# Block 2's keys: cast by Pool on landing, turned before the last weight group, that group loaded in two parts

## The chip, the cores and the metric

One Trainium2 chip, of which the kernel uses one core. The metric is the device time of one execution in microseconds (us). TensorE is called PE here, VectorE DVE, ScalarE ACT, GpSimd POOL or Pool, and SyncE SP. "SPq" and "POOLq" are the queues on which SP and Pool issue transfers (DMAs).

## What is computed

Chunked attention over 4 batches, 8 heads, 768 positions and a head width of 64, then a dense layer pair with a gate. Cut to what matters:

```python
for c in range(24):                      # chunks of 32 queries
    k_ctx = k[:, :, l_start:r_end]       # 16 positions to the left, 8 to the right
    k_full = concat([mem_k, k_ctx]); v_full = concat([mem_v, v_ctx])   # 8 memory rows ahead
    a = softmax(q_c @ k_full.T / 8)
    out[:, :, c_start:c_end] = a @ v_full
x = out.transpose(0, 2, 1, 3).reshape(3072, 512)
return (relu(x @ w_gate) * (x @ w_val)) @ w_out      # 512 -> 1536 -> 512
```

Inputs and output are float32; the kernel works in float16 and accumulates in float32.

## The kernel before, in words

The 3072 rows are cut into eight blocks of 384, two to a batch. For each block the kernel loads keys and queries (`load_kq`, L153: `kraw`, for even blocks also the memory and edge rows `kx`, then `qraw`), casts them to float16 (`cast3`, L169, into `kn` and `qn`; `cast_kx`, L175), turns them with a transposing DMA (`turn_k`, L183, into `kT`; `turn_q`, L189, into `qT`), and lets Pool copy the turned keys into bands of 120 (`bands`, L193, into `kb`: six copies for an even block). Then come four attention steps (`Step`, L231): scores on PE (L252), the exponential on ACT (L259), a mask on DVE, the values on PE (L270, which read `vb`), a division on DVE, and a transposing DMA of the result into `xT`. The dense layer of a block is twelve units `dff` (L315: four gate matmuls, a relu on ACT, four value matmuls, a product on DVE) and three output tiles.

Blocks 0 and 1 are begun together by a list written out by hand (`ORDER`, L466). After it stands the stage that the change touches (L586 to L625): 28 units for blocks 0 and 1, counted by u. Units 0 to 7 are dense units on the weight columns 512 to 1023, four for each block. Units 8 to 15 are those on columns 1024 to 1535: 8 to 11 of block 0, 12 to 15 of block 1, with a 128-column slice each, so that units 8 and 9 read columns 1024 to 1279 and units 10 and 11 columns 1280 to 1535. Units 16 to 27 are output tiles in halves (`outp_part`, L336): 16 to 21 need the first half of `w_out` (`load_wo(0)`), 22 to 27 the second (`load_wo(1)`). Into these units block 2's attention is woven: scores of steps 0 and 1 ahead of unit 12, of steps 2 and 3 ahead of unit 17 (`su`); values within units 14, 15, 19 and 20 (`vu`).

`manual_schedule` keeps each engine's instructions in program order, so the order of the text is the order of each queue. What is prepared for blocks 2 and 3 hangs on the units in the table `hook` (L591): a call that is entered at u stands behind that unit's own instructions. Ahead of the table stand a Pool write into `kraw` that waits for the weight columns up to 1023 (L586), `load_kq(2)` on SP, `cast_kx` on Pool, and `load_w(1024, 512)` on Pool: the last weight group, one DMA for `w_gate_sb` and one for `w_val_sb`, which cast to float16 on the way. Pool also issues `load_vb` (L163, block 2's values, a DMA for the rows and one for the memory rows of each step) and `load_wo` (L452, three DMAs of four row chunks each). So Pool's queue holds weight loads, value loads, band copies and output weights in one line, and what stands behind a waiting band copy waits with it.

After the 28 units a loop runs blocks 2 to 7 (L629), each with the attention of the next block woven in.

Of the kernel before, what the change touches and what calls it, by code (L numbers as in the profile page):

```python
# [15 lines left out]
def kernel(  # L16
# [57 lines left out]
    dv, pl = dve.tensor_copy, pool.tensor_copy  # L74
# [63 lines left out]
    def load3(eng, c, n, h0=0, nh=H):  # L138
        t = {"k": k, "q": q, "v": v}[c]
        i = n % 2  # L140
        dst = (vlong if c == "v" else raw[c])[:, i, h0:h0 + nh].rearrange("p h t d -> p h (t d)")
        src = bass.AP(tensor=t.tensor, offset=t[n // 2, h0, MB * i, 0].offset,
                      ap=[[R3 * D, 128], [S * D, nh], [1, R3 * D]])
        eng.dma_start(dst, src)  # L144
# [4 lines left out]
    def kx_rows(eng, b, d, t, mem, eng2=None):  # L149
        eng.dma_start(d[0:NMEM], mem[b].rearrange("h n d -> n h d"))  # L150
        (eng2 or eng).dma_start(d[NMEM:2 * NMEM], rows(t, b, MB, NMEM))

    def load_kq(n):  # L153
        load3(sp, "k", n)
        if n % 2 == 0:
            kx_rows(sp, n // 2, kx[:, (n // 2) % 2], k, mem_k)
        load3(sp, "q", n)
# [5 lines left out]
    def load_vb(n, j):  # L163
        pool.dma_start(vb_t[n % 2][0:BAND, j, :, 0:D], rows(v, n // 2, starts[NJ * (n % 2) + j], BAND))
        pool.dma_start(vb_t[n % 2][BAND:128, j, :, 0:D], mem_v[n // 2].rearrange("h n d -> n h d"))
# [3 lines left out]
    def cast3(eng, c, n, a0=0, na=HP):  # L169
        i = n % 2  # L170
        d = (kn[:, i, 0:R3].rearrange("p t a c -> p a t c") if c == "k" else qn[:, i])[:, a0:a0 + na]
        eng(d.rearrange("p a t (x d) -> p a x t d", x=2),  # L172
            raw[c][:, i, 2 * a0:2 * a0 + 2 * na].rearrange("p (a x) t d -> p a x t d", x=2))

    def cast_kx(eng, b):  # L175
        eng(kn[0:2 * NMEM, 0, R3], kx[:, b % 2].rearrange("p (a x) d -> p a (x d)", x=2))
# [6 lines left out]
    def turn_k(n):  # L183
        i = n % 2
        nt = R3 + 1 - i
        sp.dma_start_transpose(kT_t[i][:, 0:nt].rearrange("p t a c -> p (t a) c"),
                               kn[:, i, 0:nt].rearrange("p t a c -> p (t a c)"))

    def turn_q(n):  # L189
        i = n % 2  # L190
        sp.dma_start_transpose(qT_t[i].rearrange("p a t c -> p (a t) c"), qn[:, i].rearrange("p a t c -> p (a t c)"))

    def bands(n, eng, part=range(6)):  # L193
        i = n % 2
        kT, kb = kT_t[i], kb_t[i]
        early = n in EARLY

        def src(t, off, dims, sa=128):
            return bass.AP(tensor=t.tensor, offset=t.offset + off, ap=[t.ap[0], [sa, HP]] + dims)

        def dst(j, off, dims):
            return bass.AP(tensor=kb.tensor, offset=kb.offset + 128 * j + off, ap=[kb.ap[0], [NJ * 128, HP]] + dims)

        nj, TS = 3 - i, HP * 128
        P = QB // R3 - 6
        for r, t in enumerate((2, 0, 1)):
            if r in part:
                eng(dst(1, r, [[128, nj], [R3, 40]]), src(kT, TS * t + P + (r > 0), [[PP, nj], [1, 40]]))  # L208
        if 3 in part:
            if i == 0:  # L210
                eng(dst(0, 0, [[R3, 40], [1, R3]]), src(kT, 0, [[1, 40], [TS, R3]]))
            else:
                e, es, eo, ea = (ke, HP * NMEM, 2, NMEM) if early else (kT_t[0], TS, 122, 128)
                eng(dst(0, 16, [[R3, 35], [1, R3]]), src(kT, 0, [[1, 35], [TS, R3]]))
                eng(dst(0, 0, [[1, 1]]), src(e, 2 * es + eo, [[1, 1]], ea))
                eng(dst(0, 1, [[R3, 5], [1, R3]]), src(e, eo + 1, [[1, 5], [es, R3]], ea))
        if 4 in part and i == 1:
            eng(dst(3, 0, [[R3, 40], [1, R3]]), src(kT, 88, [[1, 40], [TS, R3]]))
        if 5 in part:
            if i == 0:  # L220
                eng(dst(3, 112, [[1, NMEM]]), src(kT, R3 * TS + NMEM, [[1, NMEM]]))
            if early:
                eng(dst(0, BAND, [[128, NJ], [1, NMEM]]), src(kb_t[0], BAND, [[0, NJ], [1, NMEM]], NJ * 128))  # L223
            else:
                eng(dst(0, BAND, [[128, NJ], [1, NMEM]]), src(kT_t[0], R3 * TS, [[0, NJ], [1, NMEM]]))
# [221 lines left out]
    def load_w(c0, w, only=None):  # L447
        for i, (s_, d_) in enumerate(((moe_w_gate, w_gate_sb), (moe_w_val, w_val_sb))):
            if only in (None, i):
                pool.dma_start(d_[:, :, c0:c0 + w], s_.rearrange("(c p) f -> p c f", p=128)[:, :, c0:c0 + w])  # L450

    def load_wo(x):  # L452
        for c in range(0, NDC, 4):
            pool.dma_start(w_out_sb[:, c:c + 4, HC * x:HC * x + HC],
                           moe_w_out.rearrange("(c p) f -> p c f", p=128)[:, c:c + 4, HC * x:HC * x + HC])
# [6 lines left out]
    ac = act.copy  # L462
# [117 lines left out]
    def att(n):  # L580
# [4 lines left out]

    pl(raw["k"][0:1, 0, 0, 0, 0:1], w_gate_sb[0:1, 0, 1023:1024])  # L586
    load_kq(2)
    cast_kx(pl, 1)
    load_w(1024, 512)

    hook = {  # L591
        0: [lambda: cast3(ac, "k", 2, 0, 2)],
        1: [lambda: cast3(ac, "k", 2, 2, 2), lambda: turn_k(2)],
        3: [lambda: load_vb(2, 0), lambda: load_vb(2, 1), lambda: load_wo(0)],
        4: [lambda: cast3(ac, "q", 2, 0, 2)],
        5: [lambda: cast3(ac, "q", 2, 2, 2), lambda: turn_q(2), lambda: load_kq(3), lambda: bands(2, pl)],
        8: [lambda: load_vb(2, 2), lambda: load_vb(2, 3)],
        10: [lambda: load_wo(1)],
        12: [lambda j=j: load_vb(3, j) for j in range(NJ)],
# [100 lines left out]
```

## Time and profile before

| | |
|---|---|
| seven runs | median 238.33 us, 238.05 to 241.1 |
| the profiled execution | 238.33 us, of it 236.6 us span |
| granted PE clock, mean | 0.991 |
| PE busy | 225.3 us (95% of the span) |
| DVE, ACT, POOL busy | 107.9, 113.6, 62.0 us |
| DMA | 38.62 MB, 163 GB/s over the span |
| `kn<-kraw` cast, 128x768 | POOL 827 ns (one), ACT 832 ns (median of 13), DVE 638 ns (median of 2) |
| `kT<-kn` issue on SP | 1.49 to 5.44 us, six of them |
| `w_out_sb` DMA, issue to landing | 7.5 to 14.3 us, median 10.5 |

The span runs from the first instruction to the last, and the rest of a run's time lies around it. "Busy" counts pipelined matmuls, so PE's 95% doesn't say that it works at its peak; what the time of a stretch is worth is read from the gaps in PE's timeline and from the granted clock of the stretch. A timeline row has the start, the duration, engine, line, operation and tiles, and in brackets how long the engine had been idle before it and what released it. A row of DMA queues has packets, MB and the share of 16 engines; q1 is the queue on which SP issues (q1 of the hardware kind), q0 that of Pool (software). In the trace's packet records the kinds of transfer can be told by their packet size: 256 bytes for a transposing DMA, 768 for keys and queries, 128 for block 2's values, 1024 or 512 for weights.

### The profile page before, as it was taken

How to read it: one execution, taken by the hardware profiler on the slowest of the kernel's cores; microseconds unless marked ns; L12 is line 12 of the kernel's file. 1: busy time of each engine (PE TensorE's matmuls, PEld its weight loads, DVE VectorE, ACT ScalarE, POOL GpSimd, SP SyncE). 2: the span in 40 equal slices, each digit the busy share in tenths (PEclk: the TensorE clock that was granted, in tenths of full speed). 3: DMA queues.
4: the chain of work that ended last, by engine and by line, in shares of the span. 5: the costliest groups of instructions: out<-in, count | busy, mean ns of one | idle time of the engine just before them, and what ended most of it. 6: DMA issues, size and time to landing. Idle time of an engine off the chain costs nothing.

```text
span 236.6 us, 4765 instructions
## 1 busy us (share of the span) xinstructions
PE 225.3 (95%) x1819; PEld 137.2 (58%) x1819; DVE 107.9 (46%) x231; ACT 113.6 (48%) x201; POOL 62.0 (26%) x115
## 2 busy tenths in 40 slices
PE   7989899992999999999999999999999999999994
PEld 5656666651589856645665556545654566556543
DVE  5378745440542037622764057704861276414410
ACT  2386655641354546634573465454664355133312
POOL 6589408409680321006000320005000500000000
PEclk9999999999799999999999999999999999999999
DMA  6999999999999999459972999289935901220012
GB/s 173 321 268 178 201 224 190 169 157 224 243 161 155 247 249 248 84 114 235 305 144 43 230 302 194 42 193 260 258 73 129 173 1 36 64 102 1 3 44 90
DMA packets 91883, 38.62 MB, mean 163 GB/s; under 512 B 64308, under 2 KB 89652, under 8 KB 91860
## 3 DMA queue, kind: packets, MB, share of 16 engines
q1 hardware_dynamic: 73868, 32.53, 59.4%
q0 software_dynamic: 17920, 5.77, 24.9%
q8 instruction: 14, 0.23, 0.4%
q14 instruction: 9, 0.07, 0.1%
q10 hardware_dynamic: 72, 0.02, 0.0%
HBM read 30.24 MB, written 6.29 MB: 154 GB/s over the span
## 4 chain that ended last, share of the span: by engine, by line
PE 85%; DMA 9%; DVE 2%; SPq 1%; ACT 1%; issue 1%; ACTq 0%; DVEq 0%
PE PS L300 51%; PE PS L330 19%; PE PS L339 8%; DMA qT<-qn 5%; PE PS L270 3%; DMA vraw<-in_v_dram 3%; PE PS L252 3%; DMA kraw<-in_k_dram 2%; SPq L144 1%; DVE x_big L279 1%; PE PS L288 0%; PE PS L246 0%; ACT ex L259 0%; PE PS L395 0%; DVE kb L223 0%
## 5 line engine op out<-in xcount | busy, mean ns | idle before, releaser
L311 DVE TENSOR_TENSOR gvT<-PS,g_relu 128x384 f16<-128x384 f32 x96 | 53.2, 554 | 100.6 <-PE PS L300 98.7
L300 PE MATMUL PS<-xT,w_val_sb 128*128 128x384 f16 x384 | 78.3, 328 | 0.5 <-ACT xT L291 0.5
L300 PE MATMUL PS<-xT,w_gate_sb 128*128 128x384 f16 x384 | 78.7, 329 | 0.0
L305 ACT ACTIVATE g_relu<-PS 128x384 f16<-128x384 f32 x96 | 47.2, 491 | 54.1 <-PE PS L300 42.4
L300 PEld LDWEIGHTS <-w_gate_sb 128*128 128x128 f16 x384 | 36.8, 99 | 24.9 <-issue 0.8
L300 PEld LDWEIGHTS <-w_val_sb 128*128 128x128 f16 x384 | 36.6, 98 | 23.7 <-issue 1.5
L330 PE MATMUL PS<-w_out_sb,gvT 128*128 128x512 f16 x204 | 45.8, 379 | 0.0
L208 POOL COPY kb<-kT 128x320 f16<-128x320 f16 (+1 forms) x19 | 14.8, 871 | 97.9 <-DMA kT<-kn 76.4
L330 PEld LDWEIGHTS <-gvT 128*128 128x128 f16 x204 | 19.6, 98 | 22.3
L259 ACT ACTIVATE ex<-PS 128x768 f16<-128x768 f32 x32 | 25.6, 809 | 10.9 <-PE PS L252 10.9
L333 ACT COPY o_sb<-PS 128x512 f32<-128x512 f32 x17 | 9.9, 585 | 35.0 <-PE PS L330 35.0
L279 DVE TENSOR_TENSOR x_big<-PS,rinv 96x512 f16<-96x512 f32 x32 | 22.0, 686 | 1.1
L339 PE MATMUL PS<-w_out_sb,gvT 128*128 128x256 f16 (+2 forms) x168 | 19.2, 273 | 0.0
L339 PEld LDWEIGHTS <-gvT 128*128 128x128 f16 x168 | 16.1, 98 | 2.4
L270 PEld LDWEIGHTS <-ex 128*128 128x128 f16 x256 | 12.2, 98 | 5.0 <-issue 0.7
L270 PE MATMUL PS<-vb,ex 128*128 128x66 f16 x256 | 13.4, 194 | 0.6 <-DVE x_big L279 0.5
L252 PE MATMUL PS<-qT,kb 64*128 64x96 f16 x256 | 8.9, 206 | 4.6 <-DMA qT<-qn 4.6
L252 PEld LDWEIGHTS <-kb 64*128 64x128 f16 x256 | 6.2, 95 | 10.3 <-issue 6.2
L266 DVE TENSOR_TENSOR ex<-ex,mask_int 128x768 f16<-128x768 f16 x19 | 10.3, 562 | 1.8 <-ACT ex L259 1.7
L172 ACT CAST kn<-kraw 128x768 f16<-128x768 f32 x13 | 10.8, 829 | 0.6 <-DMA kraw<-in_k_dram 0.6
L172 ACT CAST qn<-qraw 128x768 f16<-128x768 f32 x13 | 10.8, 833 | 0.0
L342 ACT COPY o_sb<-PS 128x256 f32<-128x256 f32 (+2 forms) x14 | 5.2, 372 | 10.4 <-PE PS L339 9.7
(103 smaller groups left out, 126.7 us busy)
## 6 DMA issues: line engine op xcount, KB each, us to landing
kraw<-in_k_dram SPq DMA_DIRECT2D x7, 768.0 KB
qraw<-in_q_dram SPq DMA_DIRECT2D x7, 768.0 KB
vraw<-in_v_dram SPq DMA_DIRECT2D x20, 240.0 KB
out_dram<-o_sb SPq DMA_DIRECT2D x17, 256.0 KB
w_out_sb<-in_moe_w_out_dram POOLq DMA_DIRECT2D x6, 256.0 KB, 10.5
out_dram<-o_sb SPq DMA_DIRECT2D x12, 128.0 KB
w_gate_sb<-in_moe_w_gate_dram POOLq DMA_DIRECT2D x2, 512.0 KB, 7.3
w_val_sb<-in_moe_w_val_dram POOLq DMA_DIRECT2D x2, 512.0 KB, 9.4
```

The source lines that it names most:

```text
L172: eng(d.rearrange("p a t (x d) -> p a x t d", x=2), raw[c][:, i, 2 * a0:2 * a0 + 2 * na].rearrange("p (a x) t d -> p a x t d", x=2))
L208: eng(dst(1, r, [[128, nj], [R3, 40]]), src(kT, TS * t + P + (r > 0), [[PP, nj], [1, 40]]))
L252: pe.matmul(o.rearrange("p (t c) -> p t c", t=R3), lhsT=self.kb[r, a, j, :], rhs=qT_t[i][r, a, :, PP * j:PP * j + PP], start=not self.pm, ...
L259: act.activation(self.ex[:, :, 0:QB].rearrange("p (h b) c -> p b h c", b=2), PS[:, self.sb:self.sb + 2, 0:HP * QB].rearrange("p b (h c) -> ...
L266: dve.tensor_tensor(out=e, in0=e, in1=m8, op=ALU.mult)
L270: pe.matmul(PS[:, self.pb + h // 4, VW * (h % 4):VW * (h % 4) + VW], lhsT=self.ex[:, h, :], rhs=self.vb[:, self.j, h, :], start=True, stop ...
L279: dve.tensor_tensor(out=self.x.rearrange("p (b h d) -> p b h d", b=2, h=4), in0=o[:, :, :, 0:D], in1=rb, op=ALU.mult)
L300: pe.matmul(o, lhsT=w_sb[:, f, 128 * m:128 * m + 128], rhs=xTs[n][:, f, c0:c0 + w], start=(f == 0), stop=(f == NFC - 1))
L305: act.activation(g_relu, g_ps, ACT.Relu)
L311: dve.tensor_tensor(out=gvT[n][:, m].rearrange("p (t j c) -> p t j c", t=R3, j=NJ)[:, :, j0:j0 + nj], in0=vl_ps.rearrange("p (j t c) -> p ...
L330: pe.matmul(PS[:, o], lhsT=gvT[n][:, m, 128 * t:128 * t + 128], rhs=w_out_sb[:, m, :], start=(m == 0), stop=(m == NDC - 1))
L339: pe.matmul(o, lhsT=gvT[n][:, m, 128 * t:128 * t + 128], rhs=w_out_sb[:, m, c0:c1], start=(m == 0), stop=(m == NDC - 1))
```

## The change

Pool, not ACT, casts block 2's keys, as soon as they have landed. The turning DMA of the keys is issued by SP after these casts and that of `kx`, and in Pool's queue the weight group's loads come after the casts: first columns 1024 to 1279 of both weights, then 1280 to 1535. The band copies of block 2 stand directly behind these loads, ahead of `load_vb(2, 0)`, `load_vb(2, 1)` and `load_wo(0)`. ACT casts the queries behind units 0 and 1, where it cast the keys before; behind unit 1, not 5, stand the turning DMA of the queries and the loads of block 3's keys and queries. PE's and DVE's instructions and their order stay as they were.

```diff
     pl(raw["k"][0:1, 0, 0, 0, 0:1], w_gate_sb[0:1, 0, 1023:1024])
     load_kq(2)
+    cast3(pl, "k", 2, 0, 2)
+    cast3(pl, "k", 2, 2, 2)
     cast_kx(pl, 1)
-    load_w(1024, 512)
+    turn_k(2)
+    load_w(1024, 256)
+    load_w(1280, 256)
+    bands(2, pl)
 
     hook = {
-        0: [lambda: cast3(ac, "k", 2, 0, 2)],
-        1: [lambda: cast3(ac, "k", 2, 2, 2), lambda: turn_k(2)],
+        0: [lambda: cast3(ac, "q", 2, 0, 2)],
+        1: [lambda: cast3(ac, "q", 2, 2, 2), lambda: turn_q(2), lambda: load_kq(3)],
         3: [lambda: load_vb(2, 0), lambda: load_vb(2, 1), lambda: load_wo(0)],
-        4: [lambda: cast3(ac, "q", 2, 0, 2)],
-        5: [lambda: cast3(ac, "q", 2, 2, 2), lambda: turn_q(2), lambda: load_kq(3), lambda: bands(2, pl)],
         8: [lambda: load_vb(2, 2), lambda: load_vb(2, 3)],
         10: [lambda: load_wo(1)],
```

## The prediction

> **What bounds the kernel now.** I read the chain of work that ended last first, then PE's timeline around its only DMA step after 20 us, then the granted clock there, then the timelines of SP and POOL, and the packets by queue in short windows. From 31 us to the end the chain is PE back to back, except here:
>
> ```profile
> 31.29 15.39 PE PS L300 x95
> 46.69 11.25 DMA qT<-qn
> 57.94 0.04 issue
> 57.98 0.66 PE PS L252 x16
> 58.64 4.84 PE PS L300 x20
> ```
>
> (Columns: start, duration, what.) PE needs block 2's scores ahead of unit 12 and its queries are still being turned. In PE's timeline:
>
> ```profile
> 52.58 0.81 PE L300 MATMUL PS<-xT,w_val_sb 128*128 128x384 f16 x4
> 57.98 0.66 PE L252 MATMUL PS<-qT,kb 64*128 64x96 f16 x16 [4.58 <-DMA qT<-qn]
> 58.57 1.46 PE L300 MATMUL PS<-xT,w_gate_sb 128*128 128x384 f16 x4
> ```
>
> Groups of four L300 matmuls start 0.65 apart, so the scores could have begun at 53.23: 4.75 are lost to the wait. Then the clock is down (58 to 60: 0.55; 60 to 64: 0.80):
>
> ```profile
> 58.00:60.00 2.00, 2.00 (x21) 1.16 (x21) 0.00 (x0) 0.81 (x1) 2.00 (x4) 0.55 1.10 328
> 60.00:64.00 4.00, 4.00 (x28) 2.28 (x26) 2.25 (x5) 2.17 (x4) 2.84 (x4) 0.80 1.66 241
> ```
>
> (Seventh value: granted clock.) The 16 scores take 0.59 where the next 16 take 0.45, and the 20 matmuls to unit 14's values (58.57 to 63.31) 4.74 where such a row of the chain takes 3.36. The whole loss is 4.75 + 0.14 + 1.38 = 6.27: the most that the change can give here. The keys are nearly as late; they reach Pool only at 53.10:
>
> ```profile
> 37.16 0.75 POOL L450 DMA_DIRECT2D w_gate_sb<-in_moe_w_gate_dram  x1 [0.21 <-issue]
> ...
> 53.10 2.66 POOL L208 COPY kb<-kT 128x480 f16<-128x480 f16 x3 [9.15 <-DMA kT<-kn]
> ```
>
> ```profile
> 41.05 5.44 SPq L186 DMA_TRANSPOSE kT<-kn  x1
> 46.69 4.19 SPq L191 DMA_TRANSPOSE qT<-qn  x1
> ```
>
> Issued at 41.05, landed at 53.05: 12.0, of which the DMA engines explain all. From 41 to 45 no packet of SP's queue moves; the first window below has the weights alone. Later the queues share about one for one (53 to 56: output weights and qT). And from 57.2 to 62 block 3's keys and queries run alone, though Pool issued value loads at 56.59:
>
> ```profile
> q0 software_dynamic: 749, 0.73, 120.2%
> ```
>
> ```profile
> q1 hardware_dynamic: 777, 0.20, 48.3%
> q0 software_dynamic: 709, 0.35, 85.3%
> ```
>
> ```profile
> q1 hardware_dynamic: 1982, 1.48, 107.7%
> q0 software_dynamic: 94, 0.01, 3.6%
> ```
>
> So from 38 to 68 the DMA engines are full, and what counts is which transfer is ahead of which.
>
> **The change, part by part.** The sum is made against the profiled execution: 238.33 with a span of 236.6, the same as the median of the seven runs.
>
> Pool's casts. The landing records have 15 of the 16 parts of `kraw` by 35.7 and the last at 36.91. Two casts at 827 ns (the one POOL row of this cast) and `kx` at 603 ns end at 36.95 + 1.65 + 0.60 = 39.2. So kT is issued at 39.2, 1.85 earlier than now, and the weights at 39.4 instead of 37.16, 2.2 later. ACT's two key casts (829 ns each) leave; they cost nothing now, since its relus there wait for PE anyway.
>
> Queries. ACT takes them behind units 0 and 1, where it stood free at 38.87. The last part of `qraw` landed at 40.27, so the first cast ends at 41.1 and unit 1's relu starts there, not at 39.78. PE comes back to that relu's bank at 41.53 (unit 3's gate) and to its product's at 42.18; the relu would end at 41.6, the product at 42.2. Cost 0 to 0.2, and I take 0.1. The second cast ends at 42.4: qT is issued at 42.4 instead of 46.69, and block 3's load right behind it instead of at 50.93.
>
> kT. Lower end: the quiet case. Block 3's kT, 1536 packets, was issued at 76.95 and released Pool at 80.90, its packets at 830 per us; 2048 packets make 3.95 + 0.6 = 4.6, so 43.8. Upper end: 12.0 as now, 51.2. Between: some 700 packets before the weights arrive at 40.7 (1.3 from issue to first packet, as at 37.16), the rest at the 240 to 260 per us of the window from 53 to 56: 46.3, landing near 46.9. I take 46.9, as that window has the same pair of packet sizes (512 and 256). Bands take 3.56 (53.10 to 56.66): ready at 50.5, between 47.4 and 54.8. Scores are due at 53.23.
>
> qT. 3584 packets of transposes beside 2048 of weights: the weights end at 40.7 + 2048 / 240 = 49.2, the rest of the transposes at 800 per us by 50.3, landing 50.7. Not late. Behind both of them alone it is earlier still.
>
> The rule of the Trainium skill, "DMA: Bandwidth & Descriptors", section on queues, rings and completion order, is that an engine takes turns between its queues, packet by packet. The windows from 41 to 45 and from 57.2 to 62 show it not happening for 4 us each, that from 53 to 56 shows it. By the rule kT lands near 46.9, by first come first served near 43.8; the end of the sum is the same by both.
>
> Weights. They are due at 48.03 and 48.68 (unit 8's gate and value group in PE's timeline) for the first part and at 50.63 and 51.28 for the second (unit 10). Shared as above, the first part is in by 45.4 and the second by 49.6, so nothing is lost. Lower end: alone, 2048 packets at about 400 per us (1441 in 3.5 us, from 64.5 to 68) are in by 46.3. Upper end: behind all transposes, 40.7 + 4.5 + 5.2 + 0.4 = 50.8, still in time; with block 3's 2048 packets ahead too (430 per us) 55.5, a stall of 4.3. Four issues in place of two are 1.5 more on Pool (0.75 each), under a wait for kT. The same page (anatomy of one DMA) has about 2.0 of fixed cost per DMA, which would speak against halves; by it the second part would be in at about 52 and PE would stand 1. The rows show 1024-byte packets at 0.73 MB in 4 us and 512-byte ones at 0.68 MB in 3.5, so halves cost nothing in rate.
>
> What is late next. Pool's queue behind the bands: value loads 0 and 1 (issued at 38.6 to 41.6 now), output weights (41.60 to 43.95 now). With bands done at 50.5, they are issued at 50.5 to 53.5 (four issues, 0.95 and 0.6) and 53.5 to 55.9. With the 6.27 gone, values are due at 63.31 - 6.27 = 57.0 and 58.6, and the three output pieces at 59.5, 59.9 and 60.4 (65.77 - 6.27, 0.44 apart). They now share the engines with block 3's load, which has come ahead of them. The same six transfers (weights, kT, qT, two value loads, the first output weights, block 3's keys and queries) now keep the engines full from 38.5 to 62.2: 23.7. After the change the first packet of kT moves at 39.7 and the last of the six is the third output piece. Upper end: 39.7 + 23.7 + 0.2 for smaller packets + 0.4 to land = 64.0. Lower end: each at its rate alone (kT 2.5, qT 1.9, weights 5.2, values 1.7 at 1209 per us, block 3 4.9, output 3.8) 20.0, so 60.1. I take 62.8: now the weights start slowly (150 packets from 38.5 to 40.2, where 350 would fit), and kT would run in that hole, 1.0 less; the rest of the sharing stays. So the third piece comes 2.4 after it is due, and unit 16 stands in two or three short waits, with matmuls in between. That part was reached at 66.65, and now at 62.8: gain 3.85, and 0 to 0.1 for ACT is inside the wait. The clock may fall in these waits too, which cost 1.38 after the 4.58 of idling; with matmuls in between I take 0. Bounds: 66.65 - 64.0 = 2.65 less 1.38, and 6.27. Value loads 2 and 3 and the second output half follow in the same line, near 65 and 69, and are due near 66 and 70.5.
>
> Sum: 238.33 - 3.85 = 234.5.
>
> **Rivals.** (1) Nothing is late: the output pieces come by 60.4. 238.33 - 6.27 = 232.1. For it: the rates alone; against: no stretch of mixed queues has reached them.
> (2) Block 3's load gets ahead of the weights, as it got ahead of the value loads at 57.2: the second weight part at 55.5, PE stands 4.3 at units 8 to 11, some of it also paid by the output pieces: 236.4 to 237. Against: the weights are issued at 39.4, that load after 42.4.
> (3) The turning is not earlier, since the weights still hold it: kT at 51.2, bands 54.8, and the output pieces are issued at 57.8 to 60.2; at the 7.5 of the fastest such DMA the third lands at 66.9. About 238.5.
> (4) Slower: Pool waits for kT with the output weights behind it. Their third DMA is issued 8.1 after kT (3.56 + 3.0 + 1.57), at 55.0. Now the three take 13.2 (median) to land, over all six of them 7.5 to 14.3. From 11.6 on (66.65 - 55.0) the change loses; at 14.3 it is 69.3, thus 241. For it: block 3's load is in front now. Against: the weights and both turnings, which made the 13.2, are then done.
>
> **How the numbers follow.** Forecast 0.48 (own range 232.9 to 235.7, or to 237.1 with a lowered clock), (1) 0.16, (2) 0.14, (3) 0.09, (4) 0.13. The range from 232.0 to 238.0 leaves out half of (3) and (4) and a little of (1), under 2 in 10. One per cent, about what a measurement of this kernel can tell from no change, is 2.4. Faster by more: forecast, (1) and a little of (2), 0.66. Slower by more: most of (4), 0.09. Within it: 0.25.
>
> **What would show it.** In the profile after: Pool casts two `kn<-kraw` at about 37 to 38.6 and kT is issued near 39.2; Pool's wait for kT ends between 44 and 48; PE has no gap over 1 ahead of L252 near 53, and the clock stays at 1 there; a wait of L339 on the output weights between 59 and 64. Wrong, if PE waits at L300 for weights between 48 and 53, if kT ends Pool's wait after 50, or if the third output piece lands after 66.

## The result, and the profile after

The changed kernel's median is 236.93 us over 27 runs (234.22 to 239.12); the kernel before, run beside it, has 239.9 over 64 runs (237.17 to 242.34). The ratio is 0.9869 with a 95% interval of [0.9846, 0.9892]: 1.3% or 3.1 us faster. The forecast was 3.85 us, 1.6%, just outside the interval. A ratio leaves out, on either side, the executions that lie more than 1.5% above the fastest of their kernel, while a median here is over all of them, so the two need not agree to the tenth. The profiled execution of the changed kernel took 237.24, of it 235.5 span. It lies 1.09 below the profiled execution of before (238.33), and not 3.1, because that one was 1.6 below the median of its 64 runs and this one 0.3 above its own. Executions of one kernel differ here by up to 5 us, so the profiles say where time goes, and the medians say how much.

PE's timeline around block 2's attention (start, duration, what, and in brackets the idle time before it and its releaser):

```profile
51.79 0.82 PE L300 MATMUL PS<-xT,w_val_sb 128*128 128x384 f16 x4 [0.56 <-DMA w_val_sb<-in_moe_w_val_dram]
...
53.93 0.51 PE L252 MATMUL PS<-qT,kb 64*128 64x96 f16 x16
...
60.56 0.42 PE L270 MATMUL PS<-vb,ex 128*128 128x66 f16 x8 [2.76 <-DMA vb<-in_mem_v_dram]
```

The scores stand at 53.93 with next to no wait (Pool's last band copy ended at 53.87), where they stood at 57.98 behind 4.58. Two new waits have come: a small one for the second weight part, and 2.76 ahead of unit 14's values, for block 2's first value load. The granted clock then drops as it did before the change, only later:

```profile
60.00:62.00 2.00, 1.44 (x13) 0.89 (x14) 0.89 (x2) 0.00 (x0) 1.55 (x4) 0.79 1.33 172
62.00:64.00 2.00, 2.00 (x14) 1.20 (x13) 0.83 (x3) 0.49 (x1) 2.00 (x4) 0.50 1.39 154
```

(Seventh value: the clock.) The chain of waits runs through the new stall from end to end:

```profile
39.06 11.18 DMA kT<-kn
...
50.30 2.67 POOL kb L208 x3
...
53.87 0.89 POOL vb L164
54.76 5.67 DMA vb<-in_mem_v_dram
...
60.56 0.42 PE PS L270 x8
60.98 2.24 PE PS L300 x8
63.22 0.44 PE PS L270 x8
63.66 1.18 PE PS L300 x4
```

Read it upwards: PE's values wait for a value load that Pool issued at 54.76, because Pool made the bands until 53.87, because kT took 11.18 to turn. At full clock eight L300 matmuls take 1.30, eight L270 0.25 and four L300 0.65, so the last three rows hold 0.94 + 0.19 + 0.53 = 1.66 of lowered clock.

That makes the account of the two profiled executions. Won: the 6.27 of the old stall. Lost: 0.73 for the weights (51.79 where the 0.65 step of PE's groups gives 51.06), 0.08 for the bands, 2.93 for the values (60.56 where 20 matmuls after 54.37 would have let them begin at 57.63; the 2.76 of the row count only from the end of the last matmul), 1.66 of clock. Left: 0.87. PE already stood 0.22 earlier at unit 8 in this execution (47.81 against 48.03), which makes 1.09. The first output tile (L339) starts at 64.67 against 65.77 before, and from there to the end the two run alike.

Pool casts the keys from 36.90 and `kx` till 39.03; the weights are issued from 38.99 to 41.97. SP's queue:

```profile
39.06 4.16 SPq L186 DMA_TRANSPOSE kT<-kn  x1
43.42 4.65 SPq L191 DMA_TRANSPOSE qT<-qn  x1
48.12 0.57 SPq L144 DMA_DIRECT2D kraw<-in_k_dram  x1
```

kT is issued 2 us earlier than before, and takes 11.2 in place of 12.0. Its issue alone holds SP's queue for 4.16, so qT goes out at 43.42 although ACT's second query cast ended at 40.93, and block 3's load only at 48.12. From 41 to 50 the weights (q0) and the two turnings (q1) share the engines:

```profile
q0 software_dynamic: 1816, 0.91, 91.9%
q1 hardware_dynamic: 2270, 0.57, 52.5%
```

The sharing is in bursts: 1441 packets of turning (256 bytes) in the two us from 43, and 249 in the four us from 45. By 47.3 as many have moved as kT has, 2048. But kT's sixteen parts land between 48.10 and 50.24, with qT's packets already among them; qT lands at 52.74. Then block 3's load has the engines to itself; from 52 to 56.5 this is the only queue that moves:

```profile
q1 hardware_dynamic: 1969, 1.45, 110.3%
```

The value loads were issued at 53.83 to 56.8. Their first packet moves at 56.9, and 15 of the 16 parts of the first are in by 59.2, the last at 60.42.

### The profile page after: what moved, and what is told of

Same layout as the page of the kernel before. It is cut to its first block, busy times and chain, and to the rows that moved or that the text cites. A ratio compares the mean times of both kernels' runs of the same rounds, so it can differ in the third digit from the quotient of the medians.

```text
span 235.5 us, 4768 instructions
## 1 busy us (share of the span) xinstructions
PE 225.4 (96%) x1819; PEld 137.2 (58%) x1819; DVE 108.2 (46%) x231; ACT 112.1 (48%) x199; POOL 65.2 (28%) x119
## 4 chain that ended last, share of the span: by engine, by line
PE 73%; DMA 19%; POOL 5%; SPq 1%; issue 1%; ACT 0%; POOLq 0%
PE PS L300 42%; PE PS L330 19%; PE PS L339 8%; DMA kT<-kn 5%; DMA kraw<-in_k_dram 4%; DMA w_gate_sb<-in_moe_w_gate_dram 4%; DMA qraw<-in_q_dram 4%; PE PS L270 3%; DMA vb<-in_mem_v_dram 2%; PE PS L252 2%; SPq L144 1%; POOL kb L208 1%; POOL w_val_sb L450 1%; POOL w_gate_sb L450 1%; POOL kn L172 1%
## 5 line engine op out<-in xcount | busy, mean ns | idle before, releaser
L300 PE MATMUL PS<-xT,w_val_sb 128*128 128x384 f16 x384 | 78.5, 329 | 1.1 <-DMA w_val_sb<-in_moe_w_val_dram 0.6
L300 PE MATMUL PS<-xT,w_gate_sb 128*128 128x384 f16 x384 | 78.4, 329 | 0.0
L300 PEld LDWEIGHTS <-w_gate_sb 128*128 128x128 f16 x384 | 36.7, 98 | 24.7 <-issue 0.7
L300 PEld LDWEIGHTS <-w_val_sb 128*128 128x128 f16 x384 | 36.4, 98 | 24.3 <-issue 1.1
L339 PE MATMUL PS<-w_out_sb,gvT 128*128 128x256 f16 (+2 forms) x168 | 19.2, 273 | 0.0
L339 PEld LDWEIGHTS <-gvT 128*128 128x128 f16 x168 | 16.1, 98 | 2.6 <-issue 0.2
L270 PEld LDWEIGHTS <-ex 128*128 128x128 f16 x256 | 12.4, 99 | 8.2 <-issue 4.0
L270 PE MATMUL PS<-vb,ex 128*128 128x66 f16 x256 | 13.6, 195 | 3.3 <-DMA vb<-in_mem_v_dram 2.8
L266 DVE TENSOR_TENSOR ex<-ex,mask_int 128x768 f16<-128x768 f16 x19 | 10.9, 594 | 1.9 <-ACT ex L259 1.8
L276 DVE RECIPROCAL rinv<-PS 96x8 f32<-96x8 f32 x32 | 6.3, 198 | 9.9 <-PE PS L270 9.8
L172 ACT CAST kn<-kraw 128x768 f16<-128x768 f32 x11 | 9.1, 830 | 0.4 <-DMA kraw<-in_k_dram 0.4
```

The lines of the kernel that those rows point to most:

```text
L172: eng(d.rearrange("p a t (x d) -> p a x t d", x=2), raw[c][:, i, 2 * a0:2 * a0 + 2 * na].rearrange("p (a x) t d -> p a x t d", x=2))
L266: dve.tensor_tensor(out=e, in0=e, in1=m8, op=ALU.mult)
L270: pe.matmul(PS[:, self.pb + h // 4, VW * (h % 4):VW * (h % 4) + VW], lhsT=self.ex[:, h, :], rhs=self.vb[:, self.j, h, :], start=True, stop ...
L300: pe.matmul(o, lhsT=w_sb[:, f, 128 * m:128 * m + 128], rhs=xTs[n][:, f, c0:c0 + w], start=(f == 0), stop=(f == NFC - 1))
L339: pe.matmul(o, lhsT=gvT[n][:, m, 128 * t:128 * t + 128], rhs=w_out_sb[:, m, c0:c1], start=(m == 0), stop=(m == NDC - 1))
```

## The experiments

Twelve runs, the last of them of the changed kernel itself; all times stand beside runs of the kernel before on the same chip. Base of an edit is the changed kernel unless another is named. Three theories were to be told apart. A: what is ahead in the DMA engines decides, so the rest of the gain can be had by putting block 3's load back or the value loads ahead. Its rival, B in the expectations: the engines are full in this stretch, and each reordering only makes something else late. C: kT takes 11 us only because the weights run beside it, so that both are short when run one after the other. Where an expectation names a theory, it is one of these, but for `no_w`, whose theory A is the premise of C.

**Without the last weight group** (`no_w`; Pool writes zeros in its place, so a third of the dense layer is left out).

```diff
-    load_w(1024, 256)
-    load_w(1280, 256)
+    pool.memset(w_gate_sb[:, :, 1024:1536], 0.0)
+    pool.memset(w_val_sb[:, :, 1024:1536], 0.0)
```

> The last weight group isn't loaded: Pool writes zeros into its columns instead, so a third of the dense layer is left out of blocks 0 to 7. Theory A (kT takes 11 from issue to landing because it shares the engines with the weights): kT lands by 44 to 45, the bands are ready before 49, neither scores nor values wait, the output pieces at most 0.5. Time 5.5 to 6.5 below before. The rival, that the transposes are slow by themselves: kT after 48, and the value wait stays.

Measured: 232.8, ratio 0.9718 [0.9654, 0.9782], 6.8 us faster than before. PE has no wait in the whole stretch. In Pool's timeline:

```profile
42.52 2.68 POOL L208 COPY kb<-kT 128x480 f16<-128x480 f16 x3 [0.95 <-DMA kT<-kn]
```

Issued at 38.11, kT is there at 42.5: 4.4 in place of 11.2. The old stall summed to 6.27, and the interval of this gain, 5.2 to 8.3, holds that. What takes the rest of it away is the transfer of the weights; whether that is because it runs beside the turning or because it takes its own time in the engines, this run can't tell (`turn_first` below bears on it).

**Bands back behind the values and output weights** (`bands_back`).

```diff
     load_w(1280, 256)
-    bands(2, pl)
...
         3: [lambda: load_vb(2, 0), lambda: load_vb(2, 1), lambda: load_wo(0)],
+        5: [lambda: bands(2, pl)],
```

> The band copies go back behind value loads 0 and 1 and the first output weights, to unit 5, where they stood before. Theory A: no wait at the values; kT now shares the engines with weights, values and output weights and lands at 52 to 53, so the scores wait 3 to 4 again, the clock falls again, and the time is 0.5 to 2 below before. Theory B: as the changed kernel, about 3 below before.

Measured: 240.27, ratio 1.0009 [0.997, 1.0047]. The whole gain is gone, though keys and queries are cast and turned at the same places in the queues as in the changed kernel. The queries cost 0.40 of waiting, and then PE stands three times at the output weights, with the clock down behind it:

```profile
62.28 0.61 PE L339 MATMUL PS<-w_out_sb,gvT 128*128 128x256 f16 x4 [0.51 <-DMA w_out_sb<-in_moe_w_out_dram]
64.80 0.73 PE L339 MATMUL PS<-w_out_sb,gvT 128*128 128x256 f16 x4 [1.90 <-DMA w_out_sb<-in_moe_w_out_dram]
66.44 1.01 PE L339 MATMUL PS<-w_out_sb,gvT 128*128 128x256 f16 x4 [0.92 <-DMA w_out_sb<-in_moe_w_out_dram]
```

```profile
68.00:72.00 4.00, 4.00 (x25) 2.67 (x20) 1.12 (x2) 1.81 (x3) 1.34 (x2) 0.51 1.55 192
```

Issuing the output weights 7 to 11 us earlier does not bring them sooner: Pool issues the first piece at 45.76, and the second and third only at 49.47 and 51.05, each behind an earlier transfer (2.84 for a `w_val_sb` DMA, 0.81 for a `w_gate_sb` one).

**ACT casts the keys, halves kept, turnings and bands ahead of values and output weights** (`act_cast`).

```diff
-    cast3(pl, "k", 2, 0, 2)
-    cast3(pl, "k", 2, 2, 2)
     cast_kx(pl, 1)
-    turn_k(2)
     load_w(1024, 256)
     load_w(1280, 256)
-    bands(2, pl)
...
-        0: [lambda: cast3(ac, "q", 2, 0, 2)],
-        1: [lambda: cast3(ac, "q", 2, 2, 2), lambda: turn_q(2), lambda: load_kq(3)],
-        3: [lambda: load_vb(2, 0), lambda: load_vb(2, 1), lambda: load_wo(0)],
+        0: [lambda: cast3(ac, "k", 2, 0, 2)],
+        1: [lambda: cast3(ac, "k", 2, 2, 2), lambda: turn_k(2)],
+        2: [lambda: cast3(ac, "q", 2, 0, 2), lambda: bands(2, pl)],
+        3: [lambda: cast3(ac, "q", 2, 2, 2), lambda: turn_q(2), lambda: load_kq(3), lambda: load_vb(2, 0), lambda: load_vb(2, 1), lambda: load_wo(0)],
```

> ACT casts block 2's keys behind units 0 and 1 as before, the keys are turned behind unit 1, the queries cast behind units 2 and 3 and turned behind unit 3; bands still ahead of the value loads, weights in halves, issued at 37.2. Theory A: kT is issued at 41 behind the weights, which are through by 45 or 46, and lands with fewer loads beside it at 48 to 50, not later than in the changed kernel; the bands are ready by 53.5. So Pool's cast is worth nothing: the time is that of the changed kernel within 1. The rival, that the earlier cast carries the gain: within 0.5 of before.

Measured: 236.3, ratio 0.9855 [0.9804, 0.9905], the same as the changed kernel. Pool's early cast is worth nothing that can be measured. In the profile kT goes out at 43.44, 4.4 later, and is back 1.75 earlier, since the weights, issued first, are nearly through (their last packet moves at 46.04, kT's first at 45.11):

```profile
48.55 2.67 POOL L208 COPY kb<-kT 128x480 f16<-128x480 f16 x3 [8.02 <-DMA kT<-kn]
```

5.1 from issue to Pool. Weights first, then turnings, is as good as both at once by the medians. The profile, which has no value wait, is weaker evidence: the granted clock was 0.5 from 12.32 to 19.14 in this execution and not in that of the changed kernel, and ACT's relu for u = 0 starts at 40.87 instead of 38.27. Pool's write that the loads wait for (L586) came only 0.65 later (30.93 for 30.28), so the transfers had some 2 us more.

**Only the halves** (`halves_only`; the base is the kernel before).

```diff
-    load_w(1024, 512)
+    load_w(1024, 256)
+    load_w(1280, 256)
```

> The kernel before with its last weight group in two parts of 256 columns, all else as before. Weights are not waited for there, so both theories have the time of before within 0.7; Pool issues 1.5 more, which makes the value loads and output weights 1.5 later, and these have 10 in hand.

Measured: 240.17, ratio 1.0032 [0.9996, 1.0067]: no difference. The scores still wait for the queries, 5.34 at 58.66.

**The weights whole** (`w_whole`): the two halves become `load_w(1024, 512)` again.

```diff
-    load_w(1024, 256)
-    load_w(1280, 256)
+    load_w(1024, 512)
```

> The last weight group is loaded whole again. Theory A: the value weights land near 51, so PE waits 2 to 2.5 at unit 8, but the wait for value load 0 that follows takes it up: the time is that of the changed kernel within 0.7. A rival, that the halves carry the gain: 1.5 to 2.5 above the changed kernel, near the time of before.

Measured: 237.83, ratio 0.9925 [0.989, 0.9961], between the two expectations, about 1.3 above the changed kernel with intervals that just touch. The wait at unit 8 was not seen; the profile has 0.92 at the values and 0.72 + 1.72 at the output pieces. The value weights landed at 49.29, not near 51. PE ran 1.5 later in this execution (u = 0's relu at 39.81), so the question what the halves save stays half open.

**Block 3's load put back** (`kq_late`), to unit 15, much later than unit 5, where the kernel before has it.

```diff
-        1: [lambda: cast3(ac, "q", 2, 2, 2), lambda: turn_q(2), lambda: load_kq(3)],
+        1: [lambda: cast3(ac, "q", 2, 2, 2), lambda: turn_q(2)],
...
+        15: [lambda: load_kq(3)],
```

> Block 3's keys and queries are loaded behind unit 15, not unit 1. Theory A (the value load of step 0 is late because Pool issues it behind the band copies, at 53.8, and the DMA engines then finish block 3's load, 52 to 56.9, before they begin it): value load 0 has landed by 57, PE has no gap at unit 14's values, the clock stays up, and only the third output piece is late, by under 1. Time 4.5 to 5.5 below before, 1.5 to 4 below the changed kernel. Theory B (the sum of the transfers sets the time and their order doesn't matter): the wait turns up again, at the output pieces or at unit 20's cast, and the time is that of the changed kernel within 1.

Measured: 243.74, ratio 1.0162 [1.0096, 1.0227], slower than before: theory A missed by over 8 us. The value wait fell to 0.45 as it said. But PE waits for the output pieces instead (0.26, 1.11 and 1.47), and block 3 pays:

```profile
64.64 0.60 PE L339 MATMUL PS<-w_out_sb,gvT 128*128 128x256 f16 x4 [1.47 <-DMA w_out_sb<-in_moe_w_out_dram]
...
91.70 0.51 PE L252 MATMUL PS<-qT,kb 64*128 64x96 f16 x16 [1.90 <-POOL kb L225]
```

```profile
59.42 3.23 SPq L283 DMA_TRANSPOSE xT<-x_big  x2
62.70 0.61 SPq L144 DMA_DIRECT2D kraw<-in_k_dram  x1
```

The load is issued only at 62.70, behind two `xT` turnings in SP's queue that wait for the values' results; it then shares the engines with the second output half, block 3's kT goes out at 79.51, and its scores are late at 91.70; the second output half costs 1.33 at 76.67, and the clock falls twice, from 65.42 and from 92.73, for 3.41 each. Meanwhile the engines stood empty from 52 to 54.5.

**The value loads ahead of the bands** (`vb_first`).

```diff
     load_w(1280, 256)
+    load_vb(2, 0)
+    load_vb(2, 1)
     bands(2, pl)
...
-        3: [lambda: load_vb(2, 0), lambda: load_vb(2, 1), lambda: load_wo(0)],
+        3: [lambda: load_wo(0)],
```

> Pool issues value loads 0 and 1 between the weights and the band copies. Theory A: they land by 52; kT comes up to 2 later (52), the scores wait 1.5 to 2.5, the values don't wait; the output pieces, still behind the bands, are late by 1. Time 3 to 4.5 below before. Theory B: the same within 1 as the changed kernel, about 3 below before.

Measured: 239.37, ratio 0.9926 [0.9877, 0.9975], a gain of 1.8, by the middle of the interval less than the change alone; the two intervals overlap. The value wait is gone (L270 at 57.8, unhindered), the bands are not later (52.8), and the wait is at the output pieces:

```profile
62.09 0.61 PE L339 MATMUL PS<-w_out_sb,gvT 128*128 128x256 f16 x4 [1.72 <-DMA w_out_sb<-in_moe_w_out_dram]
...
64.30 1.01 PE L339 MATMUL PS<-w_out_sb,gvT 128*128 128x256 f16 x4 [0.65 <-DMA w_out_sb<-in_moe_w_out_dram]
```

The clock falls here as well, to 0.5 from 63.20 to 70.03. With `kq_late` this fells theory A: the wait moves and doesn't go.

**Pool holds the weights until the keys are turned** (`turn_first`).

```diff
     turn_k(2)
+    pl(gate, kT_t[0][0:1, 0, 0, 0:1])
     load_w(1024, 256)
...
-        1: [lambda: cast3(ac, "q", 2, 2, 2), lambda: turn_q(2), lambda: load_kq(3)],
+        1: [lambda: cast3(ac, "q", 2, 2, 2), lambda: turn_q(2)],
...
+        7: [lambda: load_kq(3)],
```

> Pool copies one element of the turned keys, and so waits for kT, before it issues the weight loads (in halves) and the band copies; block 3's keys and queries are loaded behind unit 7. Theory C (a turning DMA and a cast load that run side by side in the engines hold each other up; one behind the other they are short): kT lands 4 to 5 after its issue, by 44; the weights, issued at 43 to 46, land by 50.5, so units 8 to 11 wait at most 1; bands ready at 49 to 50, value load 0 by 56.5, no value wait, output pieces late by up to 1. Time 4.5 to 6 below before. The rival, that only the sum of the transfers counts: the weights come 4 late at unit 8 or the output pieces 4 late at unit 16, and the time is that of the changed kernel or above it.

Measured: 239.33, ratio 0.9988 [0.9955, 1.0021]. Theory C is right in the turnings' durations, and wrong in the weights' (the last landed at 58.64, not by 50.5) and in the gain. kT comes in 4.3 (issued at 39.61) and qT lands at 46.43:

```profile
44.00 0.18 POOL L592 CAST gate<-kT 1x1 f32<-1x1 f16 x1 [4.42 <-DMA kT<-kn]
```

But the weights, issued at 44.23, now share the engines with block 3's load, which SP issued right behind qT although it stands behind unit 7 in the text, since nothing ahead of it in SP's queue waits. Its row, and the queues from 47 to 57:

```profile
44.20 0.87 SPq L144 DMA_DIRECT2D kraw<-in_k_dram  x1
```

```profile
q0 software_dynamic: 1788, 0.89, 64.5%
q1 hardware_dynamic: 2015, 1.53, 59.2%
```

That is about 190 packets per us for each, and PE stands at unit 8's gate matmuls and then at its value matmuls, for the two loads of the first half:

```profile
50.30 0.82 PE L300 MATMUL PS<-xT,w_gate_sb 128*128 128x384 f16 x4 [1.62 <-DMA w_gate_sb<-in_moe_w_gate_dram]
53.74 1.46 PE L300 MATMUL PS<-xT,w_val_sb 128*128 128x384 f16 x4 [2.62 <-DMA w_val_sb<-in_moe_w_val_dram]
```

The clock falls to 0.59 from 52 to 56. After that nothing is late, neither values nor output pieces: the whole loss was moved to the weights. Since block 3's load was not held back as meant, the run doesn't show what the weights would cost alone behind the turning.

**Block 3's casts two units earlier**, on `turn_first` (`turn_first_k3`) and on `act_cast` (`act_cast_k3`).

```diff
-        20: [lambda: cast3(ac, "k", 3, 0, 2)],
-        21: [lambda: cast3(ac, "k", 3, 2, 2), lambda: turn_k(3)],
-        23: [lambda: cast3(ac, "q", 3, 0, 2)],
-        24: [lambda: cast3(ac, "q", 3, 2, 2), lambda: turn_q(3)],
+        18: [lambda: cast3(ac, "k", 3, 0, 2)],
+        19: [lambda: cast3(ac, "k", 3, 2, 2), lambda: turn_k(3)],
+        21: [lambda: cast3(ac, "q", 3, 0, 2)],
+        22: [lambda: cast3(ac, "q", 3, 2, 2), lambda: turn_q(3)],
```

> As turn_first, and ACT casts block 3's keys behind units 18 and 19 and its queries behind 21 and 22, two units earlier each, with their turning DMAs. If block 3's keys are what is late next (PE waited 1.2 for their bands in the kernel with the filling matmuls): 0.5 to 1.5 below turn_first. If not: the same within 0.5.

> As act_cast, with block 3's casts and turning DMAs two units earlier. The same question: 0.3 to 1.2 below act_cast (236.3, 3.4 below before), or the same within 0.5.

Measured: 239.28, ratio 0.9999 [0.997, 1.0029], and 237.75, ratio 0.9876 [0.9829, 0.9923]. Neither differs from its base. What is late at block 3's scores in some profiles (0.32 in `act_cast`) is not what sets these medians.

**Matmuls of zeros ahead of unit 14's values** (`fill`): 48 more matmuls, into a bank that nothing reads, to keep PE busy through the wait.

```diff
+        if u == vu[0]:
+            mid.append(lambda: fill(48))
```

> PE runs 48 matmuls of zeros (128 columns each, about 2.7 in all) ahead of unit 14's first values, into PSUM columns that nobody reads. If the 1.7 behind the value wait are the lowered clock, as theory A has it: the wait shrinks to nothing, values start at 60.5 as before, the clock stays at 1 behind them and the time is 1 to 1.7 below the changed kernel. If the slow matmuls there come from the full DMA engines: the same time as the changed kernel, or above it where its value wait is shorter than 2.7.

Measured: 236.75, ratio 0.9885 [0.9828, 0.9942], the same as the changed kernel. In its profile the matmuls run from 57.56 to 60.24 and the clock stays up where it had fallen to 0.50:

```profile
62.00:64.00 2.00, 2.00 (x23) 1.51 (x19) 1.44 (x4) 0.48 (x1) 1.32 (x2) 1.00 2.15 158
```

The expectation took it that the value wait would lie beneath the filling. It did not: kT came at 48.36 in this execution, value load 0 was issued at 51.90 to 53.41, and its last part landed at 57.28, before the first matmul of zeros. So the filling cost its own 2.7 (57.56 to 60.24) and replaced nothing, and that the clock stayed up proves little about it. What the run does show: the slow matmuls are not the work of full DMA engines, as those are no less busy here (share 2.15 from 62 to 64, for 1.39 in the changed kernel), and the matmuls run at full speed. That idling lowers the clock is read from all the traces together, in the last section. Block 3's scores wait 1.21 at 86.05, and no gain is left in the median.

**The changed kernel again** (`after_again`, no edit), on the chip of `turn_first` and the two runs with block 3's casts earlier.

> The changed kernel once more, beside the others on their chip: 3 below before, with value load 0 landing between 57 and 60.5 from one execution to the next. By theory C it stands 1.5 to 3 above turn_first and within 1 of act_cast.

Measured: 237.67, ratio 0.9896 [0.9856, 0.9937]: below `turn_first`, not above it as theory C had it. Its profiled execution is its slowest (239.92), and shows what the upper end looks like:

```profile
60.07 0.41 PE L270 MATMUL PS<-vb,ex 128*128 128x66 f16 x8 [1.80 <-DMA vb<-in_mem_v_dram]
...
66.55 0.60 PE L339 MATMUL PS<-w_out_sb,gvT 128*128 128x256 f16 x4 [2.80 <-DMA w_out_sb<-in_moe_w_out_dram]
```

Here the third output piece is late as well. Which of the two waits carries the loss changes from one execution to the next.

No version that computes the whole beats the changed kernel by more than the intervals allow; `act_cast` equals it.

## What of the prediction held, and what did not

The ratio, put on the 238.33 of the sum, gives 235.2, inside the forecast's own range of 232.9 to 235.7. The way there held only in part. Of the three signs that the prediction named for being wrong, two came: PE waited at L300 for weights (0.56 at 51.79), and kT ended Pool's wait after 50 (50.30). The third did not (the third output piece landed at 64.51, not after 66). Of those for being right, Pool's casts, kT's issue and the scores near 53 at full clock came; the end of Pool's wait between 44 and 48 and the wait of L339 did not. So the size owes something to luck: the early kT from which it is worked out did not come, and the loss it places at the output pieces came at the value load.

**The bound.** That the old stall is worth 6.27 agrees with `no_w`, where nothing waits: 6.8, with 6.27 inside its interval. The three parts take one number from the timeline and another from the chain, but their sum comes out: from 53.23 to unit 14's values at full clock takes 3.81 (the steps of `fill`), and took 10.08.

**The casts.** Pool's end was put at 39.2 and came at 39.0; kT's issue at 39.2, and it was 39.06. The step was right and is worth nothing, as `act_cast` shows: what pays is the order in which the transfers stand, with the turnings ahead of values and output weights. `bands_back`, which puts only the band copies back behind those in Pool's queue, gives everything back.

**The queries** cost PE nothing (its groups keep their step of 0.65), less than the 0.1 taken. But qT was to be issued at 42.4, right behind its casts. These ended at 40.93, and qT went out only at 43.42, since kT's issue held SP's queue until 43.22; block 3's load followed behind qT's issue at 48.12.

**kT lands at 46.9** is the step that was off: 50.24, inside its bounds of 43.8 and 51.2. The sum lets 700 of kT's packets move before the weights come at 40.7. In the trace the weights are first (40.50), kT's first packet moves at 41.04 and the 700th at 43.33. The end of the count was nearly right all the same: 2048 had moved by 47.3, where the sum has 46.3. But it took these for kT's alone. qT, which the prediction has in its next step, is issued at 43.42; by 50, 2238 packets of 256 bytes had moved, 190 more than kT has, so qT's were among them while the slowest part of kT ended 3 us after the count says. Bands came at 53.87 for 50.5, qT at 52.74 for 50.7. That this cost the scores only 0.08 is luck: PE reached them 0.73 late because of the weights, and would else have waited 0.8 for the bands.

**Weights at 45.4 and 49.6, nothing lost.** They landed at 48.28 and 51.74, and PE lost 0.73. The upper bound of 50.8 was too low as well: the turnings' packets came in a burst from 43, the weights' from 45, and from 50 the turnings again.

**What is late next.** The prediction named the third output piece, landing at 62.8 when due at 60.4. In the profile it lands at 64.51 and is not waited for, since value load 0, due at about 57.6 and landing at 60.42, has already held PE. The prediction had the value loads' due times, 57.0 and 58.6, and their issue at 50.5 to 53.5, but gave them no landing time. With the 5.67 that one took here, bands at 50.5 would have brought the first at 57.1, only just late. `after_again` and `w_whole` have both waits, `vb_first` only the predicted one. The mechanism, that a backlog of transfers gives back part of the gain behind the scores, is what all of these show.

**The clock taken as 0**, with 1.38 as the bound, cost 1.66 in the profile. The reason given, that there would be matmuls in between, does not hold: in `vb_first` waits of 1.72 and 0.19 with matmuls between them lowered the clock, and so did 0.51 and 1.90 in `bands_back`.

**The sum.** 3.85 was forecast and 3.1 measured. In the profiled pair it is 1.1, in the medians more, and the difference lies in the executions compared. The term of 62.8 is not fully worked out either: 64.0 less the 1.0 that is named would be 63.0. A sum made against one execution can't be held to tenths where executions differ by 5.

**The rivals.** (1) needed nothing late: no median but that of `no_w` came near it. (2) did not happen here, and `turn_first` shows that it was real: waits of 1.62 and 2.62 against the 4.3 forecast, and no gain. (3) came nearly true in kT's time (50.24 of 51.2) and not in its price: the third output piece landed at 64.51, not 66.9. (4) did not come: the three pieces landed in 4.8 to 6.2 and not the 11.6 from which it decides.

Still open: why the engines share one for one at some times and in bursts at others; what sets which wait an execution gets (a lowered clock ahead of 20 us, as in `act_cast`, which sets PE back against the transfers, is one part of it); and whether block 3's load, held back until the weights are in but ahead of the values, would gain. That one was not tried.

## What to carry to other kernels

Where several transfers fill the DMA engines, an earlier issue is worth only what is queued beside it, so count the packets of everything that will be in the engines at that time. Before a stall's removal is credited, give each next transfer in its queue a due time and a landing time; the first that is late takes its share, and the clock takes some more if the waits add up, here from about 1.9 in a window of 3.41, even with matmuls between them. And an entry behind a later unit delays a transfer only if its own queue has something to wait for.

## What was not expected of the hardware

One turning of 2048 packets takes 4.3 to 4.4 us alone (`turn_first`, `no_w`) and 11.2 beside weight loads and another turning. A DMA's sixteen parts can end far apart: 2.1 us for kT in the changed kernel, and 1.2 for the value load's last part behind the other fifteen.

The granted clock falls in whole windows of 3.41 us. The trace's clock records have one of 0.5 from 61.18 to 64.59 in the changed kernel, and 6.83 long, twice that, in `turn_first`, `bands_back` and `vb_first`. In the window ahead of the first (57.77 to 61.18) PE was idle for 2.76, and busy for the rest; a wait of 1.80 (`after_again`, at 60.07) brought no drop. Laid over PE's timeline from 20 us on, such windows agree in all fourteen traces: ten had 1.90 (`kq_late`, 89.32 to 92.73) to 3.41 of idling, in one gap or in several, and the clock was 0.5 in the window after each; none with 1.81 (`halves_only`, 51.72 to 55.13) or less was followed by a drop. Where the lowered window itself had 0.65 to 1.10 of idling, a second lowered one came. The Trainium skill, "TensorE: Matmul & The Clock Gate", Part 1, tells of a free-running window of 4096 cycles (about 3.4 us) and a lowered clock after an idle one; the length agrees, and the runs add that a window need not be wholly idle.

By the Trainium skill, "DMA: Bandwidth & Descriptors", section on queues, rings and completion order, an engine goes round the queues that have work, a packet at a time. `turn_first` from 47 to 57 looks like that (1788 to 2015 packets). The kernel before from 57.2 to 62 doesn't (1982 to 94, with a value load issued at 56.59), and the changed kernel from 52 to 56.5 is less clear (1969 to none, with one issued at 53.83), since even with the engines empty 1.65 pass from that issue to the first packet (`kq_late`, 53.28 to 54.93). When a queue's packets start to count as waiting can't be told from these runs.
